# Eight of the 32 weight transfers of the second expert layer issued from POOL's queue instead of SP's

## The chip, the core and the metric

The kernel runs on one core of a Trainium2 chip. The metric is the device time of one execution in microseconds (us), as the median of several executions. The core has five engines that matter here: PE (matmuls), DVE, ACT, POOL (elementwise work) and SP (which issues transfers). Transfers between the chip's memory and the core's on-chip buffer are run by the core's 16 DMA engines, whichever queue issued them.

## The reference, cut to what matters

Three stages follow each other:

```python
attn_out = _attn_ref(...)            # gated recurrent attention, B=4, H=8, S=768, D=40
x = attn_out.transpose(0, 2, 1, 3).reshape(3072, 320)
h = x @ w_in; x = (h * sigmoid(h)) @ w_out            # 320 -> 2048 -> 320
logits = x @ phi                                      # 32 slots
d = softmax over tokens of logits;  slot_input = d.T @ x      # 32 x 320
for e in range(8):                                    # 8 experts, 4 slots each
    h = np.maximum(slot_input[e] @ w1[e], 0.0)        # 320 -> 1024
    slot_out[e] = h @ w2[e]                           # 1024 -> 320
c = softmax over slots of logits;  return c @ slot_out        # 3072 x 320
```

The change concerns `w2`, 8 experts x 1024 x 320 float32, 10.5 MB.

## The kernel before, in words

The tokens are worked through in 24 tiles of 128 (attention) and 12 blocks of 256 (MLP, logits, slot sums). The order of every step on every engine is written out by hand as a list of names, `ORDER`; each name runs the next piece of one `op_...` generator, and an engine runs its own instructions strictly in that order. So the place of a name in the list is its place in the queue of its engine.

After the last block the expert part runs once. `op_before` and `op_slot_in` (lines 865 to 920) turn the summed slots into the left operands of the experts; `op_s1` (line 922) multiplies with `w1`, `op_hT` transposes, `op_s2(y)` (line 953) multiplies with `w2` for the output columns of cut `y` (168 columns first, then 152), and `op_out` multiplies with the token weights and stores. `op_row(blk)` makes the token weights of a block; its step of line 808 is on POOL, and the transposes of line 812 on PE wait for it. `op_heat` (line 516) is idle work on PE.

`w2` lies on chip in 32 tiles `w2t[e, k]`, expert `e` (0 to 7) and quarter `k` (0 to 3) of its 1024 rows, 320 KB each as 128 partitions x 2 rows of 1280 bytes. `op_load_w2(e, k)` loads one. All 32 loads are on SP, with the last loads of `w1` (512 KB each, line 848) among them. The tiles take the place of the MLP's buffers, so a load waits until these have been read for the last time: quarter 0 and 1 lie where `wh`, `wl` and `wr` were, quarter 2 where `gT` was (read last by the transposes of line 725 of block 11 and by the logits of line 735), quarter 3 mostly where the buffers `g` were (read last by the matmuls of line 775, `op_slots(11)`, or of block 10). The transfers that SP and ACT issue take eight completion semaphores in turn, and the program lets an issue wait until the transfer that used the same semaphore before has landed. So at most eight of them are on their way.

`op_s2` reads the tiles in the order of its sixteen steps `x`: quarter `x // 4`, and within each pair of steps first the even experts, then the odd ones:

```python
for x in range(16):
    kk, z = divmod(x, 2)
    for g in range(4):
        T_.matmul(o2[o:o + 32], hT[:, kk, z, o:o + 32], w2t[2 * g + z, kk // 2][:, kk % 2, ...], ...)
```

The fourth matmul of all reads `w2t[6, 0]`; `w2t[1, 1]` is read first at `x = 5`.

The list around the loads (parts; other names left out):

```
... load_w2.2.3 ... load_w2.7.0 ... load_w2.4.1 load_w1.6 load_w1.7 ... load_w2.7.1 load_w2.5.1 load_w2.6.3 load_w2.4.3
load_w2.6.2 load_w2.4.2 load_w2.6.1 load_w2.2.2 load_w2.1.2 load_w2.3.3 load_w2.0.1 heat.5 load_w2.5.3 load_w2.0.3
row.10 row.10 row.10 row.10 load_w2.0.2 load_w2.5.2 ... slot_in (all) s1.0 s1.1 hT.0 ... row.11
load_w2.6.0 row.11 load_w2.7.2 s2.1 ... load_w2.1.1 ... load_w2.3.2 s2.1 load_w2.1.3 load_w2.7.3 ...
```

From `load_w2.2.3` on these are 26 transfers: 24 of `w2` and two of `w1`. `load_w2.6.0` is the 21st, `load_w2.1.1` the 23rd. On POOL the work among them is, in this order: line 808 of `op_row(10)` (the third of the four `row.10` above), the two memsets of `op_slot_in` (lines 902 and 908), the four small copies of `op_row(11)` (line 227, the first `row.11`), and line 808 of `op_row(11)` near the end. No transfer of the kernel before is issued by POOL.

Of the kernel before, what the change touches and what calls it, by code (L numbers as in the profile page):

```python
# [168 lines left out]
def soft_moe_mlstm(ctx: ExitStack, tc: tile.TileContext, qk, kv, o_gate, i_gate, f_gate, w_in, w_out, phi, w1, w2, cst, out):  # L169
    nc = tc.nc  # L170
    V_, G_, A_, T_, Y_ = nc.vector, nc.gpsimd, nc.scalar, nc.tensor, nc.sync
# [649 lines left out]
    w1t, w2t, pool = {}, {}, {}  # L821
# [27 lines left out]
            yield  # L849

    def op_load_w2(e, k):
        Y_.dma_start(out=w2t[e, k], in_=w2[e, 256 * k:256 * k + 256].rearrange("(c p) f -> p c f", p=128))
        yield

    wof = wo.rearrange("p a b -> p (a b)")
# [217 lines left out]
```

## Time and profile before

| | |
|---|---|
| median of 3 runs | 417.87 us (416.16 to 420.75) |
| the profiled execution | 411.2 us, of which its span 409.4 us |
| PE busy | 388.3 us, 95% of the span |
| DVE, ACT, POOL busy | 247.5, 241.3 and 120.4 us |
| moved by SP's queue | 76.55 MB |
| mean granted TensorE clock | 0.994 |

The profile is of one execution, and its times count from the start of the span. A "w" in a row stands for any of the tiles of `w1` and `w2`, since buffer numbers are left out of names. "SPq" is SP's queue: a row of it is the issue of a transfer, not the transfer. What stands in brackets behind a row is how long the engine was idle before it, and what ended that.

### The profile page before, as it was taken

The page shows a single profiled execution, that of the slowest core. Times are in us where ns is not written, and L with a number is a line of the kernel's source. Part 1 is how long each engine was busy: PE and PEld are TensorE (multiplying, and loading weights), DVE is VectorE, ACT ScalarE, POOL GpSimd, SP SyncE. Part 2 cuts the span into 40 slices and gives each one's busy share as a digit, 9 for nine tenths or more (in the row PEclk, how much of TensorE's full clock was granted, in tenths as well). Part 3 has the DMA queues.
Part 4 walks back from the last instruction along what each step waited for, and adds up shares of the span by engine and source line. Part 5 has one row for each costly group of instructions (what it writes and reads, how often), then busy time and mean ns, then how long its engine had stood idle before and what let it go on. Part 6 is the DMA issues. An engine that isn't in the chain of part 4 may idle for free.

```text
span 409.4 us, 14941 instructions
## 1 busy us (share of the span) xinstructions
PE 388.3 (95%) x6526; PEld 317.6 (78%) x6526; DVE 247.5 (60%) x569; ACT 241.3 (59%) x475; POOL 120.4 (29%) x169
## 2 busy tenths in 40 slices
PE   3999996999999999999999999999999999998796
PEld 3766984897986799967899797996878979633585
DVE  5787776756666756565774755767656554641042
ACT  3777873569487557776386756565863935430131
POOL 1265215143254452225442131442245300002000
PEclk9999999999999999999999999999999999999899
DMA  7969799477928526635571339348522198679757
GB/s 272 357 225 279 224 293 225 124 215 219 247 80 238 155 84 158 165 104 168 168 199 59 106 87 238 106 151 206 158 78 83 54 366 291 220 238 367 269 152 236
DMA packets 36992, 78.43 MB, mean 192 GB/s; under 512 B 3616, under 2 KB 18656, under 8 KB 36288
## 3 DMA queue, kind: packets, MB, share of 16 engines
q1 hardware_dynamic: 35328, 76.55, 62.3%
q8 instruction: 51, 0.84, 0.9%
q10 hardware_dynamic: 1600, 0.93, 0.8%
q14 instruction: 13, 0.11, 0.1%
HBM read 73.34 MB, written 4.13 MB: 189 GB/s over the span
## 4 chain that ended last, share of the span: by engine, by line
PE 73%; DMA 13%; DVE 5%; ACT 3%; POOL 2%; issue 2%; SPq 2%; POOLq 0%; ACTq 0%; DVEq 0%
PE h L716 39%; PE w L669 5%; DMA w<-in_moe_w 5%; PE t L735 5%; PE w L775 5%; DMA mq<-md 4%; PE w L610 3%; PE t L959 3%; PE w L643 3%; DMA qk<-in_qk 2%; PE t L689 2%; PE h L238 2%; PE t L395 1%; PE t L747 1%; PE t L516 1%
## 5 line engine op out<-in xcount | busy, mean ns | idle before, releaser
L718 ACT ACTIVATE gT<-h 128x512 f32<-128x512 f32 x96 | 56.3, 598 | 62.1 <-PE h L716 57.9
L716 PE MATMUL h<-xh,wh 128*128 128x256 f32 x384 | 83.0, 298 | 0.9 <-ACT gT L718 0.9
L716 PE MATMUL h<-xl,wh 128*128 128x256 f32 x384 | 77.5, 283 | 0.0
L716 PE MATMUL h<-xh,wl 128*128 128x256 f32 x384 | 77.3, 283 | 0.0
L725 DVE STREAM_TRANSPOSE g<-gT 128x512 f32<-128x512 f32 x96 | 63.5, 689 | 12.4 <-ACT gT L718 12.4
L716 PEld LDWEIGHTS h<-xh,wh 128*128 128x128 f32 x384 | 59.4, 191 | 11.6 <-issue 3.4
L716 PEld LDWEIGHTS h<-xh,wl 128*128 128x128 f32 x384 | 59.7, 191 | 0.0
L716 PEld LDWEIGHTS h<-xl,wh 128*128 128x128 f32 x384 | 59.7, 191 | 0.1
L716 PE MATMUL h<-xh,wr 128*128 128x256 f32 x192 | 54.3, 283 | 0.0
L716 PE MATMUL h<-xl,wr 128*128 128x256 f32 x192 | 54.2, 282 | 0.0
L594 POOL TENSOR_TENSOR xq<-qk,mq 104x512 f32<-104x512 f32 x20 | 25.8, 1288 | 45.1 <-ACT mq L303 16.5
L779 DVE SCALAR_TENSOR_TENSOR acc<-acc,vec,w 128x512 f32<-128x512 f32 x44 | 30.1, 737 | 11.5 <-PE w L775 11.5
L716 PEld LDWEIGHTS h<-xl,wr 128*128 128x128 f32 x192 | 36.8, 192 | 0.0
L716 PEld LDWEIGHTS h<-xh,wr 128*128 128x128 f32 x192 | 36.8, 192 | 0.0
L718 ACT ACT_TABLE_LOAD x27 | 34.6, 1283 | 1.9 <-DVE g L725 1.4
L570 POOL TENSOR_TENSOR arg<-mq,arg 128x512 f32<-128x512 f32 x17 | 22.8, 1340 | 21.0 <-DVE arg L564 11.6
L775 PE MATMUL w<-g,et 32*32 32x512 f32 x768 | 27.4, 599 | 0.1
L654 DVE TENSOR_TENSOR vb<-vb,w 104x164 f32<-104x164 f32 x40 | 12.6, 314 | 24.6 <-PE w L643 17.4
L669 PE MATMUL w<-vb,xq 40*64 40x41 f32 x768 | 24.4, 227 | 1.3 <-issue 1.3
L669 PE MATMUL w<-kv,xs 64*64 64x41 f32 x768 | 24.9, 229 | 0.0
L618 DVE TENSOR_TENSOR xs<-w,arg 128x512 f32<-128x512 f32 x24 | 16.4, 681 | 13.1 <-ACT arg L575 6.4
L669 PEld LDWEIGHTS w<-kv,xs 64*64 64x64 f32 x768 | 20.7, 133 | 4.4 <-issue 1.8
(217 smaller groups left out, 702.3 us busy)
## 6 DMA issues: line engine op xcount, KB each, us to landing
qk<-in_qk SPq DMA_DIRECT2D x24, 560.0 KB, 7.5
kv<-in_kv SPq DMA_DIRECT2D x24, 488.0 KB, 4.9
mq<-md SPq DMA_DIRECT2D x44, 256.0 KB, 5.3
w<-in_moe_w SPq DMA_DIRECT2D x32, 320.0 KB, 7.2
w<-in_moe_w SPq DMA_DIRECT2D x15, 512.0 KB, 6.6
cv<-in_moe_w_out SPq DMA_DIRECT2D x16, 320.0 KB, 4.9
rawi<-in_moe_w_in SPq DMA_DIRECT2D x4, 1024.0 KB, 12.0
og<-in_o_gate SPq DMA_DIRECT2D x12, 320.0 KB, 6.6
```

Of the source, the lines that this page charges most:

```text
L570: eng(f"arg.{n}", "G" if n else "V").tensor_tensor(out=arg, in0=mb.rearrange("p r (c t) -> p r c t", c=2), in1=arg, op=ALU.add)
L594: eng(f"qs.{n}", "G").tensor_tensor(out=xq[LR], in0=qkt[n % 2][LR, 0:4], in1=st[n]["qb"][LR], op=ALU.mult)
L610: T_.matmul(sc[64 * z:64 * z + 64, y, f:f + 64], qkn[o:o + D, 4 + p, t], qkn[o:o + D, 8 * y + x, t], start=True, stop=True, tile_position= ...
L618: V_.tensor_tensor(out=h2(d["xs"]), in0=d["sc"], in1=h2(d["arg"]), op=ALU.mult)
L654: V_.tensor_tensor(out=dst, in0=dst, in1=u, op=ALU.add)
L669: T_.matmul(op[64 * ch:64 * ch + 64, NP * par + p], a, vv[k][r, ch, p], start=(k == 0), stop=(k == 1), tile_position=(o, 64 * ch))
L716: T_.matmul(hp[:, z], w, x, start=(y == 0), stop=(y == 7))
L718: A_.activation(out=gt[0][:, 2 * q:2 * q + 2], in_=hp, func=AF.Silu)
L725: V_.transpose(out=us[blk][a][:, :, 4 * q:4 * q + 4].rearrange("p b c f -> p c b f"), in_=gt[0][:, 4 * q:4 * q + 4, 128 * a:128 * a + 128] ...
L735: T_.matmul(lp[32 * j:32 * j + 32], wp[:, j, 32 * q:32 * q + 32], gt[0][:, 4 * q + j], start=(q == 0), stop=(q == 3), tile_position=(0, 32 ...
L775: T_.matmul(ap[g][32 * b:32 * b + 32], d["et"][p, 4 * a + b], u[p, b].rearrange("p c f -> p (c f)"), start=(a == 0), stop=(a == 1), tile_p ...
L779: V_.scalar_tensor_tensor(out=acc[:, g], in0=acc[:, g], scalar=al[:, blk:blk + 1], in1=ap[g], op0=ALU.mult, op1=ALU.add)
```

## The change

One line, in `op_load_w2`. The list `ORDER` stays as it is.

```diff
     def op_load_w2(e, k):
-        Y_.dma_start(out=w2t[e, k], in_=w2[e, 256 * k:256 * k + 256].rearrange("(c p) f -> p c f", p=128))
+        (G_ if k > 1 and e % 2 else Y_).dma_start(out=w2t[e, k], in_=w2[e, 256 * k:256 * k + 256].rearrange("(c p) f -> p c f", p=128))
         yield
```

`Y_` is SP and `G_` is POOL. The eight transfers are those of the odd experts' quarters 2 and 3. On POOL they come in this order: `[1,2]`, `[3,3]`, `[5,3]`, then line 808 of `op_row(10)`, then `[5,2]`, the two memsets, the four copies of `op_row(11)`, then `[7,2]`, `[3,2]`, `[1,3]`, `[7,3]`, then line 808 of `op_row(11)`. Of the 26 transfers named above 18 stay on SP; `[6,0]` is the 17th and `[1,1]` the 18th of them.

## Rows read from the trace of the kernel before

**Rows 1.** The chain of waits, from 320 us on: start us, us, what.

```profile
359.93 0.37 SPq L852
...
361.88 6.93 DMA w<-in_moe_w
...
376.34 7.19 DMA w<-in_moe_w
```

**Rows 2.** Timeline of PE, 379 to 401 us: start us, us, engine, line, operation.

```profile
380.98 0.49 PE L959 MATMUL t<-w,wo 128*32 128x168 f32 x6 [0.21 <-ACT wo L948]
383.57 7.97 PE L959 MATMUL t<-w,wo 128*32 128x168 f32 x170 [2.11 <-DMA w<-in_moe_w]
```

**Rows 3.** Four-us stretches: length, busy time of the engines, PEclk, DMA share, GB/s.

```profile
332.00:336.00 4.00, 4.00 (x73) 2.34 (x66) 1.09 (x3) 0.38 (x1) 0.00 (x0) 1.00 1.04 419
356.00:360.00 4.00, 3.80 (x50) 1.92 (x53) 3.00 (x10) 0.75 (x3) 0.00 (x0) 1.00 0.01 2
...
376.00:380.00 4.00, 3.98 (x36) 1.20 (x28) 0.00 (x0) 0.54 (x1) 0.00 (x0) 1.00 1.08 366
380.00:384.00 4.00, 1.57 (x22) 0.98 (x26) 0.98 (x3) 1.31 (x7) 0.00 (x0) 1.00 1.05 358
```

**Rows 4.** Timeline of SP's queue, 346 to 382 us.

```profile
352.18 0.34 SPq L848 DMA_DIRECT2D w<-in_moe_w  x1
359.93 1.40 SPq L852 DMA_DIRECT2D w<-in_moe_w  x3
361.37 0.94 SPq L848 DMA_DIRECT2D w<-in_moe_w  x2
362.35 18.87 SPq L852 DMA_DIRECT2D w<-in_moe_w  x21
```

**Rows 5.** Waits of SP's queue, 359 to 382 us: total us, times, longest.

```profile
SPq L852 <- DMA w<-in_moe_w: 9.4, 16, 1.0
SPq L852 <- PE w L775: 6.3, 1, 6.3
```

**Rows 6.** Timeline of POOL, 338 to 400 us.

```profile
361.30 0.46 POOL L808 TENSOR_TENSOR rs<-rc,rs 128x128 f32<-128x128 f32 x1 [21.55 <-issue]
368.25 0.63 POOL L902 MEMSET wo<- 128x640 f32 x1 [6.49 <-PE t L900]
368.81 1.80 POOL L908 MEMSET wo<- 128x2048 f32 x1
370.57 1.04 POOL L227 COPY el<-lt 32x64 f32<-32x64 f32 x4
```

**Rows 7.** Timeline of PE, 358 to 364 us.

```profile
363.06 0.41 PE L812 MATMUL t<-con,rs 128*128 128x128 f32 x2
363.40 0.96 PE L880 MATMUL h<-acc,con 128*32 128x256 f32 x7
```

**Rows 8.** Timeline of DVE, 352 to 371 us.

```profile
358.59 1.30 DVE L725 STREAM_TRANSPOSE g<-gT 128x512 f32<-128x512 f32 x2
```

**Rows 9.** DMA queues and issues, 403.1 to 403.3 us: packets; KB, us to landing.

```profile
q10 hardware_dynamic: 98, 0.06, 98.3%
q1 hardware_dynamic: 12, 0.01, 10.1%
...
out<-cv SPq DMA_DIRECT2D x1, 228.0 KB, 4.5
out<-cv ACTq DMA_DIRECT2D x1, 228.0 KB, 3.6
```

**Rows 10.** One-us stretches around the start of line 959, columns as in Rows 3.

```profile
384.00:385.00 1.00, 1.00 (x28) 0.79 (x19) 0.00 (x0) 0.00 (x0) 0.00 (x0) 0.70 1.07 364
385.00:386.00 1.00, 1.00 (x18) 0.75 (x16) 0.00 (x0) 0.00 (x0) 0.00 (x0) 0.50 1.01 342
...
388.00:389.00 1.00, 1.00 (x36) 1.00 (x32) 0.00 (x0) 0.00 (x0) 0.00 (x0) 1.00 0.00 0
```

**Rows 11.** All transfers of line 852, from issue to landing.

```profile
DMA to landing us min/median/max: 3.0/7.2/8.5
```

**Rows 12.** Timeline of PE, 368 to 372.9 us.

```profile
370.61 0.62 PE L932 MATMUL h<-cv,wo 128*32 128x512 f32 x1 [0.45 <-DVE wo L915]
```

## The prediction

> **What bounds the kernel now.** I read the chain of waits first. PE holds most of it, but near the end it leaves PE for 23 us: from 359.93 to 383.5 it runs over SP's issues and the landings of `w2` transfers [rows 1]. The timeline of PE shows where it comes back: of line 959 the first six instructions run at 380.98 (each matmul counts twice there, so these are three), then PE stands for 2.11 us until a transfer has landed, and 170 more follow without a wait worth naming [rows 2]. The fourth matmul reads `w2t[6,0]`; the landing at 376.34 + 7.19 = 383.53 is its own [rows 1]. So the end hangs on when `[6,0]` lands, and PE itself would be ready at 381.47.
>
> The four-us stretches show why it lands then. From 356 to 360 the DMA engines are idle; from 372 to 384 their share is full, at 358 to 366 GB/s [rows 3]. SP's timeline and waits complete it: SP stands after 352.18 for the last readers of the old buffers (6.3 us for line 775), then issues 3, 2 and 21 transfers, and the issues of the last part wait 16 times for a landing, 9.4 us in all [rows 4, 5]. That is the limit of eight on their way: eight land in 7.19 us [rows 1], one each 0.90 us, and 327,680 bytes in 0.90 us are 364 GB/s, the rate of the stretches. The engines are full, so **bytes ahead of `[6,0]` are time**. `[6,0]` is the 21st of 26: each transfer put ahead of it costs 0.90 us, each taken from ahead of it gains 0.90 us.
>
> **The change part by part.**
>
> *What leaves SP.* Eight issues at 0.37 to 0.47 us. They hang on landings, not on SP's own pace (18.87 us for 21 issues [rows 4]), so the issue time saved is worth nothing. `[6,0]` moves from the 21st to the 17th place of SP's queue, `[1,1]` from 23rd to 18th. If the eight did not load the same engines, this would be 4 x 0.90 = 3.6 us earlier.
>
> *The first four on POOL: `[1,2]`, `[3,3]`, `[5,3]`, `[5,2]`.* POOL is idle before 361.30 [rows 6], so they wait only for their buffers. `[1,2]` lies on `gT`, which the transposes at 358.59 read until 359.89 [rows 8]; if its wait took only the part of `gT` that it covers it could run in the idle stretch up to 360, a gain of at most 0.90 us, which I leave out because the readers of the whole tile end so late. I take 359.95, the moment at which SP starts too [rows 4]. No issue by POOL stands in this trace. Below, I bound it by an issue of SP, 0.37 us; above, by the longest POOL operation near by, 1.80 us [rows 4, 6]. I take 1.0, between the two. So the four go out by about 364.5, long before SP reaches its 17th: all four land ahead of `[6,0]`. They were its predecessors on SP as well (in the list all four stand before it): 4 leave, 4 come back, sum 0.
>
> *POOL's own work behind them.* Line 808 of `op_row(10)` now stands behind three issues: 359.95 + 3.0 = 362.95, done 363.41 instead of 361.76 [rows 6]. Line 812 on PE waits for it and started at 363.06; it starts near 363.5, and line 880 and all of PE's chain behind it go 0.45 us later [rows 7]. With 0.37 us an issue nothing moves; with 1.80 it is 2.9 us. PE is then ready for the fourth matmul at 381.47 + 0.45 = 381.92, or 384.4 at worst. The cover is the wait for `[6,0]`; without it this 0.45 us would be paid in full. The memsets wait for PE's line 900 anyway and follow it 0.45 us later.
>
> *The two last `w1` tiles* go out on SP at 361.37 to 362.31 [rows 4], so up to four POOL transfers can now land ahead of them, 0 to 3.6 us. The later one landed at 361.88 + 6.93 = 368.81 [rows 1] and so lands by 372.4 at worst; line 932 starts at 370.61 and comes to it about 1.3 us in [rows 12]. At worst 0.5 us, under the same cover.
>
> *The last four on POOL: `[7,2]`, `[3,2]`, `[1,3]`, `[7,3]`.* This is what decides. On SP these stood behind `[6,0]`. On POOL they stand behind the copies that end at 371.61 [rows 6], so they go out at 371.61 + 0.45 + 1.0 = 373.1, then 374.1, 375.1, 376.1. SP meanwhile reaches `[6,0]` when its 9th of the 18 has landed; with four POOL transfers among them this is the 13th landing, as before, at 376.3 [rows 1]. So three of the four are on their way before `[6,0]` is issued, and the fourth at about the same moment; I count three ahead. They hold bytes that line 959 needs only some 4 us after its start, and they take 3 x 0.90 = **2.7 us** from the transfer that it needs first.
>
> Are they served before SP's backlog? The only place with two loaded queues is the stores at the end: at 403.1 to 403.3 the ACT queue (q10) moved 98 packets and SP's (q1) 12, and of one issue each in that stretch ACT's landed after 3.6 us, SP's after 4.5 [rows 9]. So a second queue is not kept behind SP's backlog, and nothing there looks like taking turns packet by packet; I count by issue times. The bounds of this term are 0, with none of the four ahead (-3.6 if the first four are not ahead either, the yielding rival), and 3.6 with all four.
>
> *The clock.* After the stall the granted clock was 0.50 (1.2 GHz) in the stretch of 385 and 1.00 (2.4 GHz) again at 388: 18 instructions a us against 36 [rows 10]. About 3.4 us at the lower level cost 1.7 us. A stall longer by 2.7 us may shift this into the stall (down to -1.7) or bring as much again (+1.7); I take 0.
>
> *After line 959* the tiles are all there: `[1,1]` lands 0.90 us behind `[6,0]` and is first read 34 instructions later (1.2 us at 36 a us), and `[7,3]`, issued by 376.1, has over 10 us. Stores and the last line 808 move along.
>
> **Sum.** 0 + 0 + 0 (hidden 0.45) + 2.7 + 0 = 2.7 us. The start of the 170 instructions moves from 383.57 to 386.3, the span from 409.4 to 412.1, the execution from 411.2 to 413.9. The median of the runs shown is 417.87, 6.7 above the profiled execution; I add 2.7 to it: **420.6 us**, 0.6% slower.
>
> **The rivals.**
>
> *POOL's transfers yield (not slower).* Place: the DMA engines from 361 on. If SP's queue kept its full rate and POOL's transfers moved only what it leaves, none would be ahead of `[6,0]`: 383.53 - 3.6 = 379.9, and PE would be the bound at 381.92, 1.7 us earlier than 383.57, and 3.4 earlier if the clock held too. It decides at four: with four POOL transfers ahead, the time is as before. So 414.5 to 417.9, mostly 416.2. Against it: [rows 9]; for it: only that one short stretch speaks.
>
> *The queues take turns (slower still).* If each gets half of the 364 GB/s while both have work, the last four need 4 x 0.90 x 2 = 7.2 us from 373.1 on and are through at 380.3, ahead of `[6,0]`: 4 x 0.90 = 3.6 us, 421.5. For it: full engines, and the fourth is issued as good as together with `[6,0]` anyway; against it: 98 packets to 12 [rows 9]. The Trainium skill, DMA: Bandwidth & Descriptors, section Queues, rings and completion order, has this as its rule: each DMA engine goes round the queues that have work, packet by packet. It speaks against this change, and the stores do not bear it out.
>
> *The rate rises with a second queue.* With 512 KB transfers the engines reached 419 GB/s [rows 3]. If the two queues together did that, the some 22.5 us of transfers up to `[6,0]` would shrink by 22.5 x (1 - 364/419) = 3.0 us, and 2.7 - 3.0 is no change: 417.6. Against it: the DMA share is at 1.05 and more already.
>
> *POOL becomes the bound.* If an issue takes 2.5 us or more, line 808 delays PE beyond 386.3. With 3.0: done at 369.4, line 812 6.4 us later, PE ready at 387.9; the last four go out from 381 to 390, `[6,0]` lands early, and `[7,3]` lands at 393 (3.0 is the fastest landing [rows 11]), 0.7 us after it is needed. 387.9 - 383.57 = 4.3, with that 5.0: 422.2 to 422.9; at 4 us an issue some 3 more. For it: three issues stand ahead of work that PE waits for. Against it: nothing on POOL near by takes over 1.8 us.
>
> That the change doesn't do what it says would be that POOL's transfers take semaphores of the same eight; then SP's queue would still wait for them in turn, and the result lies near no change.
>
> **How the numbers follow.** Forecast 45% (its own range 2.7 - 1.7 to 2.7 + 1.7: 418.9 to 422.3), taking turns 20% (419.8 to 423.2), yielding 13%, rising rate 8%, POOL as bound 10%, the rest 4%. About 1%, 4.2 us here, is what a measurement of this kernel can tell from no change; the runs shown lie 4.6 us apart. Slower by over 1% is most of the POOL rival, a quarter of the forecast (the clock added) and six in ten of taking turns: 0.09 + 0.11 + 0.12 = 0.32. Faster by over 1% needs yielding with the clock held: 0.07. The rest, 0.61, lies within 1%. The range reaches from 415.8, inside the yielding case, to 424.5, beyond the upper ends of the forecast and of taking turns, and the POOL rival at 3 us.
>
> **What would show it.** Right: the wait of line 959 for a transfer grows from 2.1 to about 4.4 us (386.3 - 381.92); between 373 and 381 a second queue moves bytes while the sum stays near 364 GB/s; SP's last issue of line 852 comes with `[1,1]`, at about 377; line 808 ends after 363. Wrong: line 959 runs through from 382 (yielding), or the DMA rows show over 390 GB/s with 1280-byte packets (rate), or line 812 waits for POOL by several us (POOL as bound). If the end is later although line 959 starts on time, I have missed a wait in the stores.

## The result, and the profile after

The change makes the kernel slower by about 1.2%: 419.6 us (median of 20 runs, 415.83 to 425.79) against 416.64 us for the kernel before (20 runs, 411.02 to 424.5), a ratio of 1.0119, 95% interval 1.0083 to 1.0154. A ratio here compares the faster executions of both kernels, leaving out those over 1.5% above the fastest of their kernel (five of the 20 of the changed kernel, and one of 2012.54 us of the kernel that makes the order by SP alone, below), so it is not the quotient of the medians. The forecast was 420.6 us and 0.6% slower; the sign and the time held, the size of the loss by the ratio was about double.

The profiled execution of the changed kernel has a span of 419.7 us, 10.3 more than the one before. Not all of that is the change: SP's first issue behind the stall comes at 365.41 us and not at 359.93 [rows 4], 5.48 us later, in code that is the same. The two profiles part in their first 100 us (the first instruction of line 775 starts at 102.9 and 97.2 us), and single executions of one kernel lie that far apart. So I compare stretches that begin at a common event: **from line 775** (its first 32 instructions for `slots.11`, at 358.61 us before and 364.09 after) **to the 170 instructions of line 959**. Before this is 383.57 - 358.61 = 24.96 us, after 393.63 - 364.09 = 29.54: +4.58 us, against +5.0 by the ratio.

The timeline of PE after the change (start us, us, engine, line, operation, idle time before and its releaser; here as in the fences below, lines in between are left out):

```profile
364.09 1.15 PE L775 MATMUL w<-g,et 32*32 32x512 f32 x32
368.94 0.44 PE L812 MATMUL t<-con,rs 128*128 128x128 f32 x2 [0.55 <-POOL rs L808]
386.46 0.49 PE L959 MATMUL t<-w,wo 128*32 128x168 f32 x6 [0.20 <-ACT wo L948]
393.63 8.22 PE L959 MATMUL t<-w,wo 128*32 128x168 f32 x170 [6.68 <-DMA w<-in_moe_w]
```

PE reaches line 959 as early as before, 386.95 - 365.41 = 21.54 us behind SP's start (381.47 - 359.93 = 21.54 before). Then it waits 6.68 us for a transfer where it waited 2.11 [rows 2]: the 4.57 us between them are the whole change of the stretch. The 170 instructions take 8.22 us and not 7.97: behind their start the granted clock stays at 0.50 for about 4.0 us (to about 397.6, by the stretches below), and before it was about 3.4 [rows 10].

The chain of waits of the changed kernel (start us, us, what) names the transfers:

```profile
369.56 15.19 DMA w<-in_moe_w
384.77 8.81 DMA w<-in_moe_w
393.63 8.22 PE t L959 x165
```

The landing at 384.77 + 8.81 = 393.58 is that of `[6,0]` again. Before, it was issued 16.41 us behind SP's start and took 7.19 us [rows 1]; now it is issued after 19.36 us and takes 8.81. A transfer that SP issued at 369.56 took 15.19 us. POOL's timeline has the eight transfers:

```profile
366.05 2.31 POOL L852 DMA_DIRECT2D w<-in_moe_w  x3 [20.83 <-ACT rs L804]
368.44 0.45 POOL L808 TENSOR_TENSOR rs<-rc,rs 128x128 f32<-128x128 f32 x1
372.67 0.73 POOL L852 DMA_DIRECT2D w<-in_moe_w  x1 [3.78 <-issue]
377.05 1.44 POOL L852 DMA_DIRECT2D w<-in_moe_w  x2
380.15 0.72 POOL L852 DMA_DIRECT2D w<-in_moe_w  x1 [1.66 <-issue]
383.73 0.73 POOL L852 DMA_DIRECT2D w<-in_moe_w  x1 [2.86 <-issue]
```

Three issues take 2.31 us, later ones 0.72 each. The eight landed 6.3 to 8.7 us behind their issue, the last one ([7,3], issued at 383.73) at 390.63: **all four late ones landed ahead of `[6,0]`**. The queues that moved bytes from 370 to 371 us (first two rows) and from 381.4 to 382.4 us (last two), packets, MB, share of the 16 engines, show how:

```profile
q0 software_dynamic: 46, 0.18, 49.0%
q1 hardware_dynamic: 51, 0.16, 45.7%
...
q0 software_dynamic: 60, 0.31, 85.3%
q1 hardware_dynamic: 62, 0.07, 22.7%
```

q0 is POOL's queue, q1 SP's. In these stretches the two move about equally many packets (46 to 51, 60 to 62), but a packet of POOL's queue holds 5120 bytes and one of SP's 1280 (4096 in the transfers of `w1`, which are in the first stretch). So in a stretch in which both move `w2`, POOL gets four fifths of the bytes: 0.31 MB to 0.07. The Trainium skill, DMA: Bandwidth & Descriptors, section Queues, rings and completion order, says that an engine goes round its queues packet by packet; by these rows the trace agrees. POOL's share is not four fifths all the time. From 379 to 380 us two of POOL's transfers were on their way, issued at 377.05 and 377.77, and its queue moved 2 packets:

```profile
q1 hardware_dynamic: 300, 0.36, 105.3%
q0 software_dynamic: 2, 0.01, 1.5%
```

Their packets came from about 381 us on, and the two landed at 383.42 and 384.41. So with the engines full a transfer of POOL first stands for some 4 us behind its issue and then overtakes SP's backlog in a burst.

The sum of the two does not rise. Stretches after the change (length, busy time of the engines, PEclk, DMA share, GB/s):

```profile
384.00:388.00 4.00, 2.61 (x26) 0.99 (x14) 0.97 (x3) 1.84 (x7) 0.47 (x1) 1.00 1.06 363
...
391.00:392.00 1.00, 0.00 (x0) 0.00 (x0) 0.00 (x0) 0.00 (x0) 0.00 (x0) 0.50 0.36 131
392.00:393.00 1.00, 0.00 (x0) 0.00 (x0) 0.00 (x0) 0.00 (x0) 0.00 (x0) 0.50 0.15 52
...
394.00:396.00 2.00, 2.00 (x36) 1.42 (x32) 0.00 (x0) 0.00 (x0) 0.00 (x0) 0.50 0.00 0
396.00:398.00 2.00, 2.00 (x44) 1.60 (x40) 0.00 (x0) 0.00 (x0) 0.00 (x0) 0.60 0.00 0
```

363 GB/s, as before [rows 3]. The clock falls to 0.50 (1.2 GHz) while PE stands and is back at 1.00 (2.4 GHz) within the last stretch. And from 391 to 393.6 PE stands though little is moving: 131 and 52 GB/s. The last bytes of `[6,0]` trickle in.

Of the waits from 352 to 395 us, POOL's own (engine, line, waited for: total us, times, longest):

```profile
POOL w L852 <- issue: 8.3, 3, 3.8
```

POOL's fourth, seventh and eighth issue each waited until the POOL transfer three places ahead had landed (372.35, 379.84 and 383.42 us; the issues came 0.3 us later): only three of POOL's transfers are on their way at a time. Line 812's wait for POOL is the 0.55 us of the timeline, and PE still reaches line 959 on time.

### The profile page after: what moved, and what is told of

Read it like the earlier page. It is cut to its first block, busy times and chain, and to the rows that moved or that the text cites. A ratio compares the mean times of both kernels' runs of the same rounds, so it can differ in the third digit from the quotient of the medians.

```text
span 419.7 us, 14946 instructions
## 1 busy us (share of the span) xinstructions
PE 390.9 (93%) x6526; PEld 319.5 (76%) x6526; DVE 248.5 (59%) x569; ACT 241.3 (58%) x475; POOL 126.0 (30%) x177
## 4 chain that ended last, share of the span: by engine, by line
PE 75%; DMA 15%; SPq 2%; ACT 2%; issue 2%; DVE 2%; POOL 1%; ACTq 0%; POOLq 0%
PE h L716 41%; DMA w<-in_moe_w 6%; PE w L775 5%; DMA qk<-in_qk 5%; PE w L669 5%; PE t L735 5%; PE w L610 3%; PE w L643 3%; PE t L959 3%; DMA ph<-in_moe_phi 2%; PE t L689 2%; DMA mq<-md 2%; PE t L747 1%; PE t L395 1%; PE t L516 1%
## 5 line engine op out<-in xcount | busy, mean ns | idle before, releaser
L735 PE MATMUL t<-gT,wp 128*32 128x256 f32 x384 | 24.9, 402 | 0.0
```

Of the source, the lines that this page charges most:

```text
L735: T_.matmul(lp[32 * j:32 * j + 32], wp[:, j, 32 * q:32 * q + 32], gt[0][:, 4 * q + j], start=(q == 0), stop=(q == 3), tile_position=(0, 32 ...
```

## The experiments

**Theory.** The engines that move the bytes are full, so what counts is how many bytes go ahead of `[6,0]`; POOL's transfers are issued past SP's list and overtake its backlog. **Rivals.** The queue costs by itself (every transfer on POOL delays the rest, or POOL's own work does), or landing follows the order of issue, whatever the queue. All use the stretch from line 775 to the restart of line 959: 24.96 us before, 29.54 after.

### Half of the change: the four early ones, the four late ones

```diff
-        (G_ if k > 1 and e % 2 else Y_).dma_start(
+        (G_ if (e, k) in ((1, 2), (3, 3), (5, 3), (5, 2)) else Y_).dma_start(    # first kernel
+        (G_ if (e, k) in ((7, 2), (3, 2), (1, 3), (7, 3)) else Y_).dma_start(    # second kernel
```

> Only the first four, [1,2], [3,3], [5,3] and [5,2], are issued by POOL; the last four are on SP again. Measured is the stretch from line 775's matmuls of block 11 (358.61 in the kernel before, 364.09 in the changed one) to the start of the 170 instructions of line 959 (383.57 and 393.63): 24.96 us before, 29.54 us in the changed kernel. Theory (transfers ahead of [6,0] count, and the two queues take turns by packets): [6,0] is the 17th on SP with four of POOL ahead, the 21st as before, so 25.0 us, at most 25.5 if a DMA engine lags. Rival (a transfer on POOL's queue costs by itself, wherever it stands): half of the 4.6 us, so 27.2 us.

> Only the last four, [7,2], [3,2], [1,3] and [7,3], are issued by POOL; the first four are on SP. Same stretch. Theory: all four pass [6,0], 4 x 0.90 = 3.6 us, and up to 1.0 us for a lagging DMA engine: 28.6 to 29.5 us. Rival (cost per POOL transfer): 27.2 us. Rival (POOL's early issues delay PE through line 808): as before, 25.0 us, since line 808 has no issue ahead of it here.

The timelines of PE, the early four first, then the late four:

```profile
360.96 1.15 PE L775 MATMUL w<-g,et 32*32 32x512 f32 x32
387.48 7.69 PE L959 MATMUL t<-w,wo 128*32 128x168 f32 x170 [3.42 <-DMA w<-in_moe_w]
```

```profile
361.99 1.15 PE L775 MATMUL w<-g,et 32*32 32x512 f32 x32 [0.15 <-DVE et L762]
390.77 8.99 PE L959 MATMUL t<-w,wo 128*32 128x168 f32 x170 [5.93 <-DMA w<-in_moe_w]
```

The early four give 26.52 us (+1.56), outside the 25.0 to 25.5 expected and nearer to the rival's 27.2: they are not free, though `[6,0]` has as many transfers ahead of it as before. The late four give 28.78 us (+3.82), inside the theory's range and far from a cost per transfer (which had 27.2 for both). One run each: 414.54 and 419.13 us, beside 414.29 for the kernel before. The two add up to 5.38, more than the 4.58 of the change.

### The same order, made by SP alone

If order is what costs, the kernel before must lose as much when its own list puts the late four ahead of `[6,0]`, with nothing on POOL.

```diff
-... row.11 row.11 load_w2.6.0 row.11 load_w2.7.2 s2.1 hT.1 hT.1 load_w2.1.1 ... load_w2.3.2 s2.1 load_w2.1.3 load_w2.7.3
+... row.11 row.11 load_w2.7.2 load_w2.3.2 load_w2.1.3 load_w2.7.3 load_w2.6.0 row.11 s2.1 hT.1 hT.1 load_w2.1.1 ...
```

> The kernel before, all 32 transfers on SP, with the four late ones of the change ([7,2], [3,2], [1,3], [7,3]) put directly ahead of [6,0] in the list. It makes by order alone what POOL's queue did in the change. Theory (3.6 of the 4.6 us are the order of the bytes, the other 1.0 comes with transfers on POOL): from line 775 to the 170 instructions of line 959 28.3 to 28.8 us (25.0 before, 29.5 in the change), SP's last transfer landed 27.9 to 28.1 us behind its first issue as before (29.0 in the change), ratio to before 1.007 to 1.011. Rival (the 1.0 us belongs to the order too, for instance by the longer wait): 29.3 to 29.8 us and 29 us. Second rival (order does not matter, the queue does): 25 us, ratio 1.00.

```profile
362.99 1.15 PE L775 MATMUL w<-g,et 32*32 32x512 f32 x32
385.36 0.49 PE L959 MATMUL t<-w,wo 128*32 128x168 f32 x6 [0.20 <-ACT wo L948]
391.68 7.85 PE L959 MATMUL t<-w,wo 128*32 128x168 f32 x170 [5.84 <-DMA w<-in_moe_w]
```

28.69 us, +3.73; SP's last transfer landed 28.14 us behind its first issue (27.96 before). Timed: 418.88 us against 415.62, ratio 1.0134, 95% interval 1.0064 to 1.0203, above the 1.007 to 1.011 expected, which the interval includes. The late four ahead of `[6,0]` cost 3.7 us on SP's queue and 3.8 on POOL's. That is most of the change, shown without POOL.

### The sign turned: POOL carries what line 959 needs first

```diff
+        (G_ if (e, k) in ((6, 0), (1, 1)) else Y_).dma_start(
```

> The kernel before with two other transfers on POOL: [6,0] and [1,1], the ones that line 959 waits for first and next, and none of the eight of the change. A test of the sign: if POOL's transfers pass those that SP has issued, the same mechanism must now help. Theory: POOL issues the two behind its copies of line 227, 13 us behind the matmuls of line 775, and they land 6.5 to 7.5 us later; line 959 starts without a wait, 22.4 to 23.2 us behind line 775 (25.0 before, 29.5 in the change), and waits further on, for [7,2], until 26 to 27.3 us behind it; the end of its 176 comes at 31 to 33 us (32.9 before). Rival (transfers land in the order of their issue, whatever the queue): also early, since they are issued early, but not before 16 to 18 others, 24 us or later. Second rival (any transfer on POOL delays the rest): line 959 starts at 25 us or later.

```profile
373.53 1.60 POOL L852 DMA_DIRECT2D w<-in_moe_w  x2
```

```profile
360.56 1.15 PE L775 MATMUL w<-g,et 32*32 32x512 f32 x32
382.94 3.00 PE L959 MATMUL t<-w,wo 128*32 128x168 f32 x80 [0.20 <-ACT wo L948]
386.45 0.76 PE L959 MATMUL t<-w,wo 128*32 128x168 f32 x10 [0.51 <-DMA w<-in_moe_w]
389.10 3.76 PE L959 MATMUL t<-w,wo 128*32 128x168 f32 x86 [1.89 <-DMA w<-in_moe_w]
```

Line 959 starts 22.38 us behind line 775 without a wait for a transfer. `[6,0]`, issued by POOL at 373.53, landed at 379.88; two transfers that SP had issued at 372.04 and 372.93 landed behind it, at 381.19 and 381.98. The later waits end 28.5 us behind line 775, later than the 26 to 27.3 expected, and the 176 instructions end after 32.30 us (32.9 before). One run took 411.99 us, beside 414.23 for the kernel before. The same queue, and the stretch is shorter by 2.58 us and not longer: the sign hangs on what the queue overtakes. Most of the gain goes again into the later waits; 0.6 us is left at the end of line 959.

### The list by need, with and without POOL

From `load_w2.2.3` on, the list's 26 loads are put into the same places roughly in the order in which they are first read (`[6,3]`, `[5,3]` and `[7,3]`, whose buffers are free early, stand ahead of quarter 2), once with all transfers on SP and once with the change's eight on POOL:

```
7.0 6.0 4.1 1.1 w1.6 w1.7 7.1 5.1 0.1 6.1 6.3 5.3 7.3 2.2 0.2 4.2 6.2 1.2 3.2 5.2 7.2 2.3 0.3 4.3 1.3 3.3
```

> The changed kernel with the same eight on POOL, but the 26 loads of the list in another order: those whose buffers are free early and that are read first (quarters 0 and 1, [6,0] second, then [6,3], [5,3], [7,3]) ahead of those that wait for block 11. Theory (the order of the bytes decides, not the queue): [6,0] lands before PE needs it, no wait of line 959 for a transfer over 0.5 us, the stretch is PE's own 22.9 us, and the clock does not fall before line 959: 6.5 us and more less than the changed kernel. Rival (the queue costs by itself): a wait of 2 us or more stays at line 959.

> The kernel before (all loads on SP) with the list order of e3_pool_by_need. Theory: as there, no wait over 0.5 us at line 959, the stretch is 22.9 us, and with the clock kept the end comes 2.1 + 1.7 = 3.8 us earlier than in the kernel before, 1 us more or less. If the queue mattered beyond the order, it would differ from e3_pool_by_need by more than 1 us.

One execution each took 409.29 us (on POOL) and 406.99 us (on SP), beside 414.29 for the kernel before, and 22.36 and 22.37 us from line 775 to line 959. The totals differ by more than the 1 us expected, the stretch does not. Both were then timed:

> The same kernel as the single look at all 32 transfers on SP with the list ordered by need, now timed in rounds. Theory (the order of the bytes sets the end): line 959 starts without a wait for a transfer and its clock stays at the full level, so 2.1 us of wait and about 1.7 us of half clock go, and 959 is reached some 2.5 us earlier from line 775 (22.4 us in place of 25.0): ratio to before 0.980 to 0.990. Rival (the 406.99 of the single look was a lucky run): 0.995 to 1.0.

> The same list by need, with the eight transfers on POOL as in the change, timed in rounds. Theory (the queue itself costs nothing where the order is right): from line 775 to 959 22.4 us again, the ratio to before within 0.004 of that of the kernel with all transfers on SP. Rival (POOL's transfers cost by themselves, by the 16 completion marks that they spread): 1 to 2 us above it, a ratio 0.003 to 0.006 higher.

PE with all on SP, then with eight on POOL:

```profile
358.28 1.15 PE L775 MATMUL w<-g,et 32*32 32x512 f32 x32
380.65 6.32 PE L959 MATMUL t<-w,wo 128*32 128x168 f32 x176 [0.20 <-ACT wo L948]
```

```profile
358.18 1.15 PE L775 MATMUL w<-g,et 32*32 32x512 f32 x32
380.55 6.32 PE L959 MATMUL t<-w,wo 128*32 128x168 f32 x176 [0.20 <-ACT wo L948]
```

22.37 us in both, no wait for a transfer, and 6.32 us for all 176 instructions at the full clock. All on SP: 408.72 us against 412.49 for the kernel before, ratio 0.9882 (0.9841 to 0.9922), the fastest version here. Eight on POOL: 409.27 us, ratio 0.9914 (0.9860 to 0.9968). The ratios differ by 0.003, within both intervals: whether POOL costs 1 us more there is not settled by the totals; in the stretch it costs nothing, since no transfer is waited for.

### What repeats

> The changed kernel once more, to see what of it repeats. Theory: from line 775 to the 170 instructions of line 959 28.3 to 29.7 us; the 3.6 us of the order repeat, and the last 1.0 us, by which the slowest of the 16 marks of [6,0] was late, follows where the 16 KB packets of the instruction queue fall: it may be anything from 0 to 1.5 us, with the spread of the marks. Rival (POOL's queue spreads the marks by itself): the spread of the marks of [6,0] is again 3.4 us and the stretch 29.3 to 29.8 us.

> The kernel before once more, to see what of it repeats. Theory: from line 775 to the 170 instructions of line 959 24.9 to 26.2 us, the spread of the 16 marks of [6,0] 1.7 us or, if a 16 KB packet of the instruction queue falls on an engine that is already the last, up to 3.1 us. Rival (only transfers on POOL spread the marks): 1.7 to 1.8 us and 24.9 to 25.1.

The kernels before and after, one more execution each, in this order:

```profile
358.95 1.15 PE L775 MATMUL w<-g,et 32*32 32x512 f32 x32
383.86 1.61 PE L959 MATMUL t<-w,wo 128*32 128x168 f32 x34 [2.05 <-DMA w<-in_moe_w]
```

```profile
363.42 1.15 PE L775 MATMUL w<-g,et 32*32 32x512 f32 x32
393.00 8.24 PE L959 MATMUL t<-w,wo 128*32 128x168 f32 x170 [6.73 <-DMA w<-in_moe_w]
```

These executions took 410.07 and 420.94 us in all, and the stretches 24.91 and 29.58 us (24.96 and 29.54 the first time): the stretch repeats within 0.05 us, so the 0.9 us by which the change exceeds the order alone (29.54 - 28.69) repeats too. Each transfer sets 16 marks on its semaphore, and its tile counts as landed at the last. For `[6,0]`, in us behind SP's first issue:

```
                     first   8th    15th   last
before               21.83  22.21  23.47  23.59
before, again        21.38  21.60  23.25  23.54
late four, SP alone  25.11  25.27  26.81  27.33
late four on POOL    25.47  25.78  27.18  27.42
early four on POOL   21.92  22.55  24.69  25.16
after                24.77  25.23  26.85  28.17
after, again         25.71  26.41  28.08  28.22
```

I had put the 0.9 us down to where the 16 KB packets of the instruction queue happen to fall, with a spread that differs from run to run. The spread does differ (3.4 and 2.5 us), but the last mark does not (28.17 and 28.22), so that theory is not supported; nor is its rival, a constant spread (and the kernel before, again, has 2.2 us where that rival had at most 1.8). The 0.9 us come with the early four on POOL (they cost 1.56 us alone, and the late four alone end at 27.42). They are not more bytes ahead of `[6,0]`: by its last mark the engines had moved 8.94 MB both in the change and in the order by SP alone. With the early four alone the first mark comes about as early as before and the last 1.6 us later, and 8.36 MB had moved by then against 7.94: bytes of later transfers move while the last part of `[6,0]` is still out. So the 16 parts of a transfer run further apart; by what mechanism stays **open**.

### Half of the reserve, and ACT's queue

```diff
-    nc = bacc.Bacc("TRN2", target_bir_lowering=False, num_devices=1, dynamic_dma_scratch_size=1024)
+    nc = bacc.Bacc("TRN2", target_bir_lowering=False, num_devices=1, dynamic_dma_scratch_size=512)
```

> The change with half of the reserve for the descriptors of POOL's transfers (512 for 1024), everything else as in the change. Theory (this reserve is what lets only three of POOL's transfers be on their way): at most two, and rather one, at a time; POOL's second or third issue waits until the first has landed, and at the late ones each waits for the one before; the last of the eight is issued later than [6,0], so fewer pass it, and from line 775 to 959 it is 26.5 to 28.8 us unless POOL, stopped at its issues, becomes the bound (its line 808 comes late by 4 us or more, and then 29.5 or more). Rival (the limit of three is something else): three at a time, 29.2 to 29.8 us.

```profile
367.48 0.87 POOL L852 DMA_DIRECT2D w<-in_moe_w  x1 [20.81 <-ACT rs L804]
374.51 0.73 POOL L852 DMA_DIRECT2D w<-in_moe_w  x1 [6.17 <-issue]
381.30 0.73 POOL L852 DMA_DIRECT2D w<-in_moe_w  x1 [6.06 <-issue]
382.10 0.45 POOL L808 TENSOR_TENSOR rs<-rc,rs 128x128 f32<-128x128 f32 x1
```

```profile
382.60 0.69 PE L812 MATMUL t<-con,rs 128*128 128x128 f32 x2 [12.78 <-POOL rs L808]
401.41 3.86 PE L959 MATMUL t<-w,wo 128*32 128x168 f32 x104 [0.20 <-ACT wo L948]
```

One transfer at a time: the second is issued 0.31 us behind the landing of the first (374.20), the third 0.31 us behind that of the second (380.99). So the reserve sets the number, three with 1024 and one with 512. Line 808 now stands behind two landings, PE waits 12.78 us for it at line 812, and the run took 428.71 us: the forecast's rival "POOL becomes the bound", made real by the wait at the issue. The stretch is 35.89 us (line 775 starts at 365.52), on the branch of the expectation that had 29.5 or more.

```diff
-        (G_ if k > 1 and e % 2 else Y_).dma_start(
+        (A_ if k > 1 and e % 2 else Y_).dma_start(
```

> The change with ACT's queue in place of POOL's, everything else as in the change. ACT's and SP's packets should both be of 1280 bytes, so two queues in turn get a half of the rate each and not four fifths and one fifth. Theory (turns by packets, and the spread of one transfer's 16 completion marks comes from POOL's software queue): the late four still end ahead of [6,0] where ACT issues them early enough, since a half of the rate moves four in 7.2 us; the marks of [6,0] spread by about 1.8 us as before and not 3.4; from line 775 to 959 27 to 28.6 us. Rival (any second queue spreads the marks): spread over 3 us, 28.6 to 29.6. Second rival (only POOL's large packets overtake): [6,0] lands as before, 25.0 to 26.

```profile
364.81 1.46 ACTq L852 DMA_DIRECT2D w<-in_moe_w  x3
393.76 0.37 ACTq L852 DMA_DIRECT2D w<-in_moe_w  x1
```

```profile
384.92 1.06 PE L932 MATMUL h<-w,wo 128*32 128x512 f32 x1 [4.21 <-DMA w<-in_moe_w]
397.01 5.25 PE L959 MATMUL t<-w,wo 128*32 128x168 f32 x96 [2.48 <-DMA w<-in_moe_w]
```

424.25 us and 33.50 us from line 775 (363.51) to line 959, outside all three expectations, and no test of the turns. SP's first issue (367.87) came only when ACT's first transfer had landed (367.86); the two share the eight semaphores, so the queues hardly ran side by side. Five `w1` transfers went out on SP behind 367.87, where the kernel before has two behind its stall, the early four on ACT went ahead of them, PE waited at line 932, and the late four left ACT only behind that wait. What it shows is how much `w1` depends on being early: 5.3 us of waits at line 932.

## Why the prediction was right, and where not

**The time, 420.6 us against 419.6: in part luck.** The forecast added 2.7 us to 417.87, the median of three executions; over 20 the kernel before has 416.64 (the medians of 20 lie 2.96 us apart, the ratio and the traces give 4.8 to 5.0). A base 1.2 us too high and a term 2.1 us or more too small partly cancel.

**SP's issues worth nothing: right.** In the changed kernel too the issue of `[6,0]` hangs on a landing: it comes at 384.77, and the transfer that SP issued at 369.56 landed at 384.75.

**The first four, sum 0: mis-sized.** Alone they cost 1.56 us; in the change about 0.9 stays on top of the late four. As many transfers were ahead of `[6,0]` as forecast, but with transfers on POOL the last marks come later, and the sum had no term for that.

**An issue by POOL, 1.0 us taken: 0.72 to 0.87 measured,** and, not forecast, three issues waited 8.3 us in all for landings. It did no harm here, since what waited behind them was the memsets and the late four; with half of the reserve it was the largest term.

**Line 808 and PE, 0.45 us hidden: right in the sum, with luck in the steps.** Line 808 moved by 1.66 us against SP's start (3.03 for 1.37) and ended 3.48 us behind it, as forecast, because POOL's first issue came 0.6 us later than taken and the three were as much shorter (2.31 us for 3.0). Line 812 moved by 0.40 us, PE's arrival at line 959 by 0.00. So the chain behind line 812 did not go later, as the forecast had it, and the cover was not the wait for `[6,0]`: in the kernel before line 880 waits 0.40 us for ACT's copy of line 781, and behind a later line 812 it no longer does.

**The `w1` tiles, hidden: right, but not by its working.** The later tile landed 13.0 us behind SP's start (378.43), past the forecast's worst of 12.5. No wait for a transfer stands at line 932 even so: it reads that tile in its 16th matmul, some 3 us in and not 1.3.

**The last four, three ahead of `[6,0]`, 2.7 us: the term that failed in size.** All four were ahead. The count went by issue times that had `[6,0]` issued 16.4 us behind SP's start, at the 13th landing, the 9th of SP with four of POOL. But what overtakes SP's backlog also delays the landings that SP's issues wait for: six of POOL's had landed by SP's 9th, so it was the 15th landing, most of SP's transfers took 10 to 15 us, and `[6,0]` was issued only after 19.4 us, 1.0 us behind the last of the four. By order alone four cost 3.73 us, against 3.6 in the rival's working. What led to three was the judgement that nothing looked like taking turns, from 98 packets against 12 [rows 9]. That stretch was too short for it. Half a microsecond later in the kernel before, from 403.6 to 403.8, the same two queues stand the other way round:

```profile
q1 hardware_dynamic: 89, 0.05, 93.0%
q10 hardware_dynamic: 15, 0.01, 13.8%
```

A fifth of a microsecond showed a burst of one queue, and I read it as a rule; what SP's queue had ready to move then, no row shows. The rival that had the mechanism (the queues take turns, 3.6 us, 421.5) had 20%; its price was right, though it too had the turns at half and half from the issue on, and they were four to one, in bursts some 4 us behind it.

**The clock, 0: nearly right,** +0.25 us (8.22 for 7.97 us of the 170 instructions). Both of the forecast's cases came at once: the lower level lasted twice as long (390.8 to 397.6), and some 2.9 us of it fell into the stall.

**Sum.** 2.7 forecast; 3.6 to 3.7 for the order, 0.9 with transfers on POOL, 0.25 of clock: 4.8 us, and 5.0 by the ratio. The forecast's other marks: the wait of line 959 grew to 6.7 us and not 4.4; the sum of the rates stayed at 363 GB/s, as said; SP's last issue came 21.2 us behind its first (386.56) and not 17. The yielding rival, the rising rate and POOL as the bound did not occur, and POOL's transfers do not take SP's eight semaphores: in the trace each of the eight has one of its own.

## What to carry to other kernels

Where the DMA engines are full, moving transfers to a second queue bought no rate here (363 GB/s with one queue and with two); it changes the order in which bytes arrive, and that order has to be set by what the next instruction reads first. Before splitting a list over queues, ask of each moved transfer what it will overtake: here four late tiles ahead of one early tile cost 3.7 us, and the same queue with the early tile on it took that tile's wait away, for 0.6 us at the end of line 959. The better step was to order the one list by need (ratio 0.9882).

## What the runs showed of the hardware

- POOL's queue moves the same `w2` transfer in packets of 5120 bytes where SP's uses 1280; where the two moved equally many packets, it got four fifths of the bytes (0.31 to 0.07 MB in 1 us). With full engines its packets begin some 4 us behind the issue (issued at 377.05 and 377.77, 2 packets from 379 to 380 us).
- The reserve for POOL's descriptors limits its transfers on the way: three of 320 KB with 1024, one with 512, and POOL itself stands at the issue until the oldest has landed.
- A packet of 16 KB of the instruction queue takes about 1.1 us on one engine, and in two runs one mark of 16 became late as one ran: with half of the reserve the gap from the 15th to the last mark went from 0.05 to 1.17 us across the one at 386.63, and in the kernel with ACT's queue from 0.15 to 1.39 us across the one at 392.18. That the packet is the cause is inferred from the times.
